# A state-space layer with a gated feed-forward, forward and backward, on one core: the next magnitudes loaded once the current ones are read, and the written order made anew

## The chip, the core and the metric

The kernel runs on one NeuronCore of a Trainium2 chip. TensorE (PE) multiplies matrices, with its weight loads (PEld) beside it; VectorE (DVE), ScalarE (ACT) and GpSimd (POOL) work on tiles of 128 partitions; SyncE (SP) issues DMAs, as ScalarE and GpSimd can too. Each engine runs its own list of instructions in order and waits on semaphores. PSUM holds what TensorE writes until another engine copies it out; such a copy is called an evacuation here. The metric is the device time of one execution in microseconds, the median of several.

## The reference

The forward pass is a layer norm, a state-space convolution of length 2048 per channel (512 channels, 128 states each) by FFT, a feed-forward layer of width 1792 that gates it, and a residual. The kernel returns the output and, from `jax.vjp`, eleven gradients for `grad_out`.

```python
def _A_ref(u, A_re, A_im, B_re, B_im, C_re, C_im, log_dt, Dskip):
    dt = jnp.exp(log_dt)[:, None]
    logdA = dt * (A_re + 1j * A_im)
    dB = dt * (B_re + 1j * B_im)
    P = jnp.exp(logdA[:, :, None] * l[None, None, :])
    K = jnp.einsum("dn,dnl,dn->dl", Cc, P, dB).real
    ...
    Yf = Uf * Kf[None, :, :, :]
    return y + u * Dskip[None, None, :]

def _B_ref(x, w1, w2):
    return jnp.einsum("bsf,fd->bsd", _silu(jnp.einsum("bsd,df->bsf", x, w1)), w2)

xn = _layernorm(x)
return x + _A_ref(xn, ...) * _silu(_B_ref(xn, B_w1, B_w2))
```

## The kernel before

Everything is written as generators ("streams"). Each `yield` ends a step. `PLAN` (L27 to L46) is seven strings of letters, one for each stage; `play` (L120) goes through a string and takes one step of the stream of that letter. So the strings are the program order of every engine and every DMA queue. `SLOTS` (L49) says which buffer of a pool each new tile takes, and `WAYS` (L65) says for each evacuation, stream by stream, whether ScalarE ("A", `nc.scalar.copy`, L116) or VectorE ("D", L117) makes it. The pool `pf` has three PSUM buffers, for the feed-forward, the turned tiles and the weight gradients, `pc` has two, for the convolution and the state-space part; a tile that takes a buffer waits until the tile before it there is evacuated.

The streams that matter here:

- Start. `gen_setup_loads` (1) loads the rows of x in five pieces, `gen_weight_loads` (0) W1 in three and W2 in two, `gen_param_loads` (p) loads the six parameter matrices by transposing DMAs. `gen_layer_norm` (6) makes xn on VectorE, `gen_rows_turned` (J) turns it on TensorE (L138), `gen_ffn_fwd` (F) multiplies by W1 (L763) and W2 (L780).
- Magnitudes. `gen_magnitudes` (7) computes |A| to 30 powers for every channel and stores it to DRAM as `Md`, eight pieces of 480 KB, one for each half (64 channels) of each of four blocks. Half number 2b+h is piece 2b+h.
- `gen_phases` (P) makes the phases of a half: two instructions on VectorE (L577, L580) and one on ScalarE (`sn`, L584).
- `gen_powers` (Q) is the function that is changed. For a half it loads the magnitudes into one part of `ds` (L597), multiplies phases by magnitudes in four multiplies (L611; two steps), which fill the table `E` (also in `ds`), the first powers in `Y` and a small `H`; it stores `E` to DRAM as `Ed` (L613), makes the other powers of `Y` in six multiplies and sums (L622, L624, L626), and stores `Y` as `Yd` (L628). `E`, `H` and the magnitudes have one buffer each; `Y` has two, one for each h.
- `gen_kernel_rows` (R) multiplies the table by C on VectorE (L646) and the powers by that on TensorE (L652), puts the rows of the convolution's kernel together in `KE` (L663, L667) and copies them to `Kb` in eight DMAs, one for each group of 16 channels (L683).
- `gen_conv_x` (X) and `gen_conv_fwd` (C) transform the input and the kernel (`dft_fwd`, L397: products L406, turns L420 to the tile `dB`, products L430 and L434) and multiply the spectra.
- Later stages: the backward convolution (D, B), the feed-forward gradients `gen_da` (A, L1168) and `gen_dx` (x, L1192), the state-space gradients (N, Y, V, T, S, Z), the weight gradients `gen_dw2` (w, L1231, with its turned tiles t) and `gen_dw1` (v, L1260, with the transposing loads of `dh_tok`, g, L1246), and the closing layer norm (i, k, m: loads L1280 and L1282, VectorE L1301 to L1323, ScalarE L1308). `gen_ssm_fold` (N) makes the tile `G21` of `pc` in two banks (L962) that ScalarE copies out (L965) before `gen_ssm_v` (V, L1020) can be read on. `gen_ssm_grads` (Z) stores its six results `gout` from GpSimd's queue (L1119).

Of the kernel before, what the change touches and what calls it, by code (L numbers as in the profile page):

```python
# [45 lines left out]
""".replace("\n", "").split("/")  # L46


SLOTS = dict(x.split("=") for x in """  # L49
fp.XT=01010101;pf.pf=012010210210120120102102012012012012012012012012012102102101210210210210210210202012012012012012102  # L50
102102102101202012102102102102102102120202102101210210210210210210212012012012012102102102102120120120102102120201201201
2020120210210201201201210;fp.hT=0101010101010101;dft.w8=21301203121030230123012320312301;pc.pc=0101011010101011010101010
101011010101010110101010101010101010101010101010101010101010101010101011010101010010101010101010101010101010101010101010
101010101010101010101010101010101010101010101010101101010101010101010101101010101010101011010111010101010101010010101010
10101010101010101;fp.ob=0101010;tbl.tv=01011101110101010101101010101110;tbl.ts=01010101010111010010101000100010;tbl.W=01
010110101110100101;dft.t4=010010101010;gate.g=30124567;gate.S=01;da.doT=01010101;da.dhT8=01201201;dftb.w8b=1010;da.dhT6=
10101010;go.go_s=01010101;go.go_r=010101;go.go_g=01010101;go.go_x=01201201;da.pd_s=101010101010;sb.YT=2012012012012012;s
b.Eb=01010101;sb.Gb=01010101;sb.Vb=0101010101010101;sb.Tp=0101010101010101;sb.Sa=1010;fw.h_in=01201201201201;fw.a_tok=10
101010101010;fw.o11=01201201201201;sb.g_acc=0101;fw.dh_tok=0120120;fw.o10=1010101;lw.pd_l=012301;lw.Gt=01230123;lw.m=010
101;lw.o1=12031203  # L60
""".replace("\n", "").split(";") if x)

WAYS = """J=DDADADAA;  # L65
F=ADAAAAAAADDAAADAAADAAAAAAAAAAADAAAAAAAAAAAAADDAAAAADAAADADDDAAADADDDAAAA;
X=AAAAAAAAAAAAAAAAAAAAAAAAAAAAAAAA;
U=AD;
R=AAAAAAAAAAADAADAAADAAADAAAAAAAAA;
C=ADDADAAAAAAAAAAAAAAADDAAAAAAAADDAAAAADAAAAADADAAADADDDADAAAAAAAA;  # L70
W=DDDDDDDDDDDDDD;
D=AAAADDAAAAAAAAADAAADAAAAAAAAAADAADAAAAAA;
d=DDADDAAD;
B=AAAAAAAAAAADAADAADAAAAAAAAAAAAAADAAADAAAAADAADAAAAAAADAA;
x=AADAADADDADA;
V=DAAADAAAAAAAAAAAADADAAADAAAAAAAAAAAAAAAAAAAAAAAAAAAAAAAAAAAAAAAA;
Y=DAAAAAAA;
w=DADADDAAAAAAAA;
v=AAADAADAAAADADAAAAAAAAAAAAAA"""


class Placed:
# [17 lines left out]
NX = len(X_EXP)  # L100
# [488 lines left out]
def gen_powers(k, b, h):  # L589

    nc, tbl = k.nc, k.tbl
    TT = nc.vector.tensor_tensor
    qe = lambda ap: ap.rearrange("p e c (q a) -> p e c q a", a=4)
    eq = lambda ap: ap.rearrange("p c q e a -> p e c q a")
    tab = k.ds[:].rearrange("p t d -> p (t d)")
    mag = tab[:, 5376:5376 + 64 * NX].rearrange("p (e d) -> p e d", d=64)
    nc.sync.dma_start(tab[:, 5376:5376 + 64 * NX], k.Md[2 * b + h])  # L597
    yield
    E = tab[:, 0:2688].rearrange("p (c q e a) -> p c q e a", c=2, q=16, a=4)
    Y = k.Y[h]  # L600
    H = tab[:, 7360:7744].rearrange("p (c q e a) -> p c q e a", c=2, q=16, a=4)
    k.E[b, h] = E
    for x0 in (0, 15):
        sn = k.sn.pop((b, h, x0))
        if x0 == 0:
            parts = ((E[:, :, :, 1:16, :], 0, 15),)
        else:
            parts = ((E[:, :, :, 16:NE, :], 0, 5), (Y[:, :, :, 1:8, :], 5, 12), (H, 12, 15))
        for o, i0, i1 in parts:
            m = mag[:, x0 + i0:x0 + i1, :].unsqueeze(2).to_broadcast([P, i1 - i0, 2, 64])  # L610
            TT(out=eq(o), in0=qe(sn[:, i0:i1]), in1=qe(m), op=ALU.mult)  # L611
        yield
    nc.sync.dma_start(k.Ed[b, h], tab[:, 0:2688])  # L613
    yield
    shp = [P, 16, 3, 8, 4]
    lo = lambda c: Y[:, c, :, 0:8, :].unsqueeze(2).to_broadcast(shp)
    hi = lambda c: H[:, c].unsqueeze(3).to_broadcast(shp)
    out = lambda c: Y[:, c, :, 8:32, :].rearrange("p q (k m) a -> p q k m a", m=8)
    for c, (x, y), op in ((0, ((0, 0), (1, 1)), ALU.subtract), (1, ((0, 1), (1, 0)), ALU.add)):
        m1 = tbl.tile(shp, BF16, name="m1", tag="tv", bufs=2)  # L620
        m2 = tbl.tile(shp, BF16, name="m2", tag="ts", bufs=2)
        TT(out=m1[:], in0=lo(x[0]), in1=hi(x[1]), op=ALU.mult)  # L622
        yield
        TT(out=m2[:], in0=lo(y[0]), in1=hi(y[1]), op=ALU.mult)  # L624
        yield
        TT(out=out(c), in0=m1[:], in1=m2[:], op=op)  # L626
        yield
    nc.sync.dma_start(k.Yd[b, h], Y[:].rearrange("p c q j a -> p (c q j a)"))  # L628
    yield
# [437 lines left out]
def gen_ssm_grads(k, b, sb):  # L1067
# [262 lines left out]
def kernel(ctx, tc, A_u, A_A_re, A_A_im, A_B_re, A_B_im, A_C_re, A_C_im, A_log_dt, A_Dskip, B_x, B_w1, B_w2, grad_out,  # L1330
# [53 lines left out]
    with ExitStack() as es_s:  # L1384
# [91 lines left out]
```

## Time and profile before

| | |
|---|---|
| three runs | 580.93, 579.06, 580.84 us; median 580.84 |
| the profiled execution | 584.31 us, of which 582.5 us are its span |
| granted TensorE clock, mean | 0.983 |
| DMA | 144.49 MB, mean 248 GB/s |
| magnitude load `ds<-Md` | eight of 480 KB on SyncE's queue, 6.2 us median from issue to landing |

The page of the profile lists, for the slowest core, the busy time of each engine, the span in 40 slices (a digit is the busy share in tenths), the chain that ended last, the costliest groups of instructions, and the DMA issues. A row of instructions reads: start, duration, engine, line, operation, out<-in, shapes, count, and in brackets the idle time of the engine just before it and what ended it. A row of waits reads: who waited, for whom, total, times, longest. "issue" there means that no releaser was found for the wait. SPq rows are DMA issues, with the time that SyncE's queue took to issue them.

### The profile page before, as it was taken

To read this page: it belongs to the slowest core of one execution; us is meant where nothing else is said; L and a number is where in the kernel's file an instruction comes from. 1 tells how busy PE (TensorE), PEld (TensorE's weight loads), DVE (VectorE), ACT (ScalarE), POOL (GpSimd) and SP (SyncE) were. 2 spreads that over 40 slices of the span, in tenths; PEclk is the share of its full clock that TensorE was granted. 3 is DMA by queue.
4 is the path that set the end of the run, shared out by engine and by line. 5 is a ranking of instruction groups with operands and counts; after the bars stand their busy time and mean duration, and the time that the engine had idled before them with its cause. 6 is when DMAs were issued, how large, how long until landed. Compare 5 with 4: busy or idle time off the path is not lost.

```text
span 582.5 us, 14494 instructions
## 1 busy us (share of the span) xinstructions
PE 528.8 (91%) x5983; PEld 395.7 (68%) x6008; DVE 521.9 (90%) x820; ACT 445.8 (77%) x542; POOL 77.6 (13%) x164
## 2 busy tenths in 40 slices
PE   0589998899999899999999999997899999999786
PEld 0355876586778675886587766765678797867564
DVE  7999998999999769999999999866999999991993
ACT  5989989899999669998888876752567686743563
POOL 4351101010101020000000000000000120333121
PEclk9989999999999999999999999999999999999798
DMA  8987897898977999779789999998899989999592
GB/s 245 283 317 194 260 245 252 266 291 220 356 218 253 322 283 365 230 254 289 243 258 289 262 297 282 222 182 220 227 230 220 211 240 251 198 227 235 119 270 97
DMA packets 156643, 144.49 MB, mean 248 GB/s; under 512 B 83488, under 2 KB 132896, under 8 KB 153504
## 3 DMA queue, kind: packets, MB, share of 16 engines
q1 hardware_dynamic: 146816, 120.74, 77.2%
q0 software_dynamic: 6640, 19.67, 10.0%
q10 hardware_dynamic: 3120, 3.15, 1.8%
q8 instruction: 47, 0.77, 0.5%
q14 instruction: 20, 0.16, 0.1%
HBM read 62.78 MB, written 59.25 MB: 209 GB/s over the span
## 4 chain that ended last, share of the span: by engine, by line
PE 45%; DMA 6%; DVE 4%; SPq 3%; issue 2%; ACT 1%; ACTq 0%; DVEq 0%
PE ps_w L1231 7%; PE ps_da L1168 7%; PE ps_w L1260 6%; PE ps_dx L1192 6%; DMA dh_tok<-DHd 4%; PE pt_t L138 3%; PE psS L1057 3%; PE ps_v L1020 3%; PE ps_i L451 2%; PE ps_i L464 2%; SPq L495 1%; PE ps_s L434 1%; PE ps_s L406 1%; DMA go_x<-in_A_u_dram 1%; PE pt_f L420 1%
## 5 line engine op out<-in xcount | busy, mean ns | idle before, releaser
L116 ACT CAST dA<-ps_s 128x1024 bf16<-128x1024 f32 x88 | 87.8, 1030 | 8.2 <-PE ps_s L434 3.8
L763 PE MATMUL ps_h<-XT,W 128*128 128x256 bf16 x448 | 59.6, 282 | 11.2 <-ACT hT L116 6.3
L116 ACT CAST Vb<-ps_v 128x672 bf16<-128x672 f32 x59 | 41.7, 728 | 24.2 <-PE ps_v L1020 15.7
L1260 PE MATMUL ps_w<-dh_tok,xn 128*128 128x256 bf16 x448 | 55.0, 280 | 5.6 <-ACT o L116 3.3
L763 PEld LDWEIGHTS <-W 128*128 128x128 bf16 x448 | 43.5, 101 | 19.6 <-issue 12.6
L1168 PE MATMUL ps_da<-doT,W 128*128 128x256 bf16 x448 | 56.1, 273 | 0.0
L1260 PEld LDWEIGHTS <-xn 128*128 128x128 bf16 x448 | 44.2, 100 | 12.6 <-issue 6.3
L1192 PE MATMUL ps_dx<-W,dhT 128*128 128x512 bf16 x224 | 51.2, 380 | 0.0
L780 PE MATMUL ps_o<-W,aT 128*128 128x512 bf16 x212 | 49.3, 379 | 1.6 <-ACT aT L771 0.6
L1231 PE MATMUL ps_w<-YD,a_tok 128*128 128x512 bf16 x211 | 49.1, 379 | 0.7
L116 ACT CAST dB<-ps_i 128x1024 bf16<-128x1024 f32 x39 | 39.0, 1021 | 11.2 <-PE ps_i L451 11.2
L1168 PEld LDWEIGHTS <-W 128*128 128x128 bf16 x448 | 41.4, 98 | 8.2 <-issue 2.1
L1171 DVE TENSOR_TENSOR dhT<-ps_da,dhT 128x512 bf16<-128x512 f32 x56 | 37.4, 682 | 5.1 <-PE ps_da L1168 5.0
L780 PEld LDWEIGHTS <-aT 128*128 128x128 bf16 x224 | 20.9, 98 | 26.0 <-ACT aT L771 2.6
L1192 PEld LDWEIGHTS <-dhT 128*128 128x128 bf16 x224 | 21.3, 98 | 24.2 <-issue 1.5
L1231 PEld LDWEIGHTS <-a_tok 128*128 128x128 bf16 x224 | 21.7, 98 | 23.5 <-ACT a_tok L1222 0.2
L477 DVE TENSOR_TENSOR cm<-sp_in,dA 128x2048 bf16<-128x2048 bf16 x24 | 29.3, 1220 | 3.9 <-ACT dA L116 2.8
L1020 PE MATMUL ps_v<-Gb,YT 128*128 128x168 bf16 x256 | 27.1, 238 | 5.6 <-ACT Vb L116 3.5
L584 ACT ACTIVATE sn<-V 128x1920 bf16<-128x1920 int16 x16 | 29.1, 1818 | 3.6 <-DVE ds L611 2.5
L116 ACT CAST o<-ps_w 128x256 bf16<-128x256 f32 (+1 forms) x34 | 14.7, 436 | 21.6 <-PE ps_w L1260 13.7
L1222 ACT ACTIVATE a_tok<-pt_t 128x1024 bf16<-128x1024 bf16 x28 | 29.0, 1039 | 2.7 <-PE pt_t L138 2.6
L1146 ACT ACTIVATE dhT<-dhT 128x2048 bf16<-128x2048 bf16 (+1 forms) x16 | 27.5, 1719 | 3.5 <-DMA dhT<-Hd 3.5
(242 smaller groups left out, 1238.9 us busy)
## 6 DMA issues: line engine op xcount, KB each, us to landing
Yd<-YD SPq DMA_DIRECT2D x8, 1024.0 KB, 5.5
sp_in<-Ud SPq DMA_DIRECT2D x8, 1024.0 KB, 7.7
h_in<-Hd SPq DMA_DIRECT2D x14, 512.0 KB, 5.2
Ed<-ds SPq DMA_DIRECT2D x8, 672.0 KB, 5.6
Eb<-Ed SPq DMA_DIRECT2D x8, 672.0 KB, 5.5
Hd<-hT POOLq DMA_DIRECT2D x8, 512.0 KB, 7.6
Ud<-dA SPq DMA_DIRECT2D x8, 512.0 KB, 9.7
KXd<-dA SPq DMA_DIRECT2D x4, 1024.0 KB, 4.1
```

Source lines behind the costliest of these rows:

```text
L116: return self.nc.scalar.copy(out=out, in_=in_)
L477: TT(out=t2[:], in0=b[:, :, gs], in1=a[:, 1:2, gs].to_broadcast([P, 2, n, P]), op=ALU.mult)
L584: nc.scalar.activation(out=sn[:, 0:n], in_=low, func=ACT.Sin, scale=-2 * PI_LO / 2.0 ** PB)
L763: nc.tensor.matmul(out=ps[:, j], lhsT=k.W1[:, dk, ft * P:ft * P + P], rhs=XTv[:, :, dk, :], start=(dk == 0), stop=(dk == DK - 1))
L780: nc.tensor.matmul(out=ps[:], lhsT=aT[:, ft, t * P:t * P + P], rhs=k.W2[:, ft, :], start=(ft == 0), stop=(ft == FT - 1))
L1020: nc.tensor.matmul(out=ps[:, u, 168 * c:168 * c + 168], lhsT=YT[:, c, q + u, :], rhs=Gb[:, q0 + q + u].rearrange("p w x -> p (w x)"), star ...
L1168: nc.tensor.matmul(out=ps[:, j], lhsT=k.W2[:, ft, dk * P:dk * P + P], rhs=dTv[:, :, dk, :], start=(dk == 0), stop=(dk == DK - 1))
L1171: nc.vector.tensor_tensor(out=dh[:, i0:i0 + 2, :], in0=ps[:], in1=dh[:, i0:i0 + 2, :], op=ALU.mult)
L1192: nc.tensor.matmul(out=ps[:], lhsT=dhs[ft // 8][:, ft % 8, t * P:t * P + P], rhs=k.W1[:, :, ft * P:ft * P + P], start=(ft == 0), stop=(ft ...
L1222: yield from turned(k, lambda t: h[:, t], k.T, a, lambda out, in_: k.nc.scalar.activation(out=out, in_=in_, func=ACT.Silu))
L1231: nc.tensor.matmul(out=ps[:], lhsT=at[:, t, :], rhs=k.do[:, t, :], start=(t == 0), stop=(t == k.T - 1))
L1260: nc.tensor.matmul(out=ps[:], lhsT=k.xn[:, t, dk * P:dk * P + P], rhs=dh[:, t].rearrange("p j n -> p (j n)"), start=(t == 0), stop=(t == k ...
```

## The change

In `gen_powers` the load of the magnitudes moves. Before, every half began with the load of its own. Now the first half alone does so, and every half but the last loads the next half's magnitudes as soon as its own multiplies (L611) are written, ahead of the store of the table `Ed`. The number of loads and their sizes are the same, and so is the number of steps.

```diff
-    nc.sync.dma_start(tab[:, 5376:5376 + 64 * NX], k.Md[2 * b + h])
-    yield
+    load = lambda i: nc.sync.dma_start(tab[:, 5376:5376 + 64 * NX], k.Md[i])
+    if (b, h) == (0, 0):
+        load(0)
+        yield
     E = tab[:, 0:2688].rearrange("p (c q e a) -> p c q e a", c=2, q=16, a=4)
...
             TT(out=eq(o), in0=qe(sn[:, i0:i1]), in1=qe(m), op=ALU.mult)
+        yield
+    if (b, h) != (3, 1):
+        load(2 * b + h + 1)
         yield
     nc.sync.dma_start(k.Ed[b, h], tab[:, 0:2688])
```

Beside it all seven strings of `PLAN` are new, and `SLOTS` and `WAYS` with them. The first lines of each:

```diff
 PLAN = """
-221325p5325515566767571677777766647701JJ70p7775076F6377766F76pF774770J786877J3F773177F06p6676643643F86853376F174F76FFFF6
...
+222315555166p567155737777617777p63677J710360734777p07J6760F3p67677J64FF7687J7F667F86676261F873776F03778FFFF47FF66667FF76
...
-WAYS = """J=DDADADAA;
...
+WAYS = """J=DDAADDAD;
```

Followed through the generators, letter by letter, the strings give every engine's list. Each list has the same steps as before (574 with work for TensorE, of which 477 stand in the same order; evacuations on VectorE 93 before, 94 now). The places of which the text below speaks, as the lists have them (half n is written Md*n*, Ed*n*, Yd*n*; da, dx, v, G are groups of L1168, L1192, L1020, L962):

| place | before | after |
|---|---|---|
| SyncE, start (x: pieces of the rows) | Ar, x0, x1, W1.0, x2, W1.1, Ai, W1.2, Br, Bi, W2.0, x3 | x0, Ar, x1, x2, Ai, W1.0, x3, W1.1, Br, Bi, W1.2, W2.0 |
| VectorE before the first xn | table steps (5), rows 0 and 1 of the statistics, L515, one table step | table steps (3), the two rows, table steps (3), L515 |
| SyncE, halves 1 to 3 | Ud0, Ed1, Yd1, load Md2, turn X1 (2), Kb0 (8), Ed2, Yd2, load Md3, Ud0 back, Ud1, Ed3, Yd3, load Md4 | Ud0, load Md2, Ed1, Yd1, turn X1 (2), Kb0 (8), load Md3, Ed2, Ud0 back, Ud1, Yd2, load Md4, Ed3 |
| SyncE, halves 6 and 7 | load Md6, KXd1, Ed6, turn X3 (2), Kb2 (8), Yd6, load Md7, Sd1, Ed7 | load Md6, ..., KXd1, load Md7, Ed6, turn X3 (2), Kb2 (8), Yd6, Sd1, Ed7 |
| TensorE, second fold | dx6.0, ..., G1.0, da7.5, dx6.1, v2.0, da7.6, G1.1, v2.1 | dx6.0, G1.0, da7.4, G1.1, da7.5, dx6.1, v2.0, v2.1 |
| evacuations of v2.0, v2.1 | ScalarE, both | VectorE, both |
| TensorE, closing (dW1 groups w1, dW2 groups w2, turned tiles T) | w1_3.2, w1_3.3, T11, T11, w1_4.0, w1_4.1, w2_10, T12, w1_4.2 | T11, w1_3.2, w1_3.3, w2_10, T11, w1_4.0, w1_4.1, T12, w1_4.2 |
| ScalarE, closing | ..., o10 of w1_4.0, T11, first L1308, o10 of w1_4.1, o11 of w2_10 | ..., o10 of w1_3.3, first L1308, o11 of w2_10, T11, o10 of w1_4.0 |
| SyncE, closing (pairs of `dh_tok` f.0, f.1) | ..., 5.0, h13, L1280 and L1282 for rows 3 and 4, 5.1, row 5, 6.0, 6.1 | 5.0, rows 0 to 2, 5.1, rows 3 and 4, 6.0, row 5, 6.1 |

More of the change, by code (lines that the diff above doesn't have):

```diff
@@ new lines @@
+347674678F73F586F47688758/XXJPFJFFFXXXFXFXPXFQPFPFXFFPFFPFFFFPPFFFFF9FQJUUXFQQXJPXXQRQQXQQQFRFQPRRFRXFXFRXXPRFFPRRFFFPQF
+UQRXXFFQFXFQFQPQQFUQFQFQRFFXFQXPXFPFXQRPXFRXRPRRRRRXPQRPFFFRPFRRRRRXFRFRXCQXXXQFXQQXQRQFQQRFQXXFRRUXFPRRQCRPFCPPFCFCCFCC
+PCFQFJFQCQCCFQQFCQPFQCRRCCQQRCCFPXCXFQPCPJFXRFCFXRCFCPFCXFXFFFRCFRFQFRCFRFFRXFCXPCRRQQXFXRFCQCFRQFQQQRCRCRRQCQRCRRRCFQPC
+XCXRRFCRRJPPXPXXRQJFXRPXQCQFQXFXFXQPQCRRQFQPQCPCRXFCCRFFQFCCCFCPCCFFRFFUFFCQCFFFCRCRCFCQRCFCCCRJCCRCQCXPXFXPCQCXRPCRCQXC
+FXFCRQQPCRQPJCFRQCRCRFXCQPQCCXFFRFRXRQRXRFFXQCXRCPFFCRRFCFCRRCRFFFXXCQQCFCCFQFQQXFRXRRFRCCQCFUFXCQCQRCCQCRRRCRJCCRQRRCRJ
@@ new lines @@
+CRCCCRUCFCRCCRCRRFCRRFCC/CFCFCGGCGFGCCCGFFFCCFGCCCGGCGFCCFFCFGFCCCCGCFGGFWCCGFGCCCGHFCFCGHFCCFCGGFHCFCCGGCFCGCGCGCCCFCWG
+CHWHWHWHCWCCCWWCDDGWCHCLCWMCWWWWDDWWDWDDWDWWWWLMWCDWDDWDLGDMDLMLWWM/DDEDDDDaaasdooEdWDdoDdDABAADooAABADsBDADAAaDAABAlABB
+BBDDAABABAsDDAAaoBAABBBADODABBABOEBBABABDBBoDDBxsBDBBxBoBxBAAdBBBOoBAsAlDBOABxBdOEDBDoOlBxBaDxOoOBxOxODDBBDxxDBlABBsxBoB
+ABBxoBAADBOAAOaBaoDBBBBBoDDBaAABBDAoDAdDBBAADBAdBABBAEAABABsBBAAODOABoOABBDBABEADODoDOxoDBAlDsOBoADDOAxAdBDDBOAoAdBADABB
+BoxBAoOADsDxBABOOBBADBDOlaBoAAxOBDBDooxBBxBBaBAOxDxBABDoBDOsODBDADxBEBOBAAOdBOBoBABxxOAoAaBdABAoBBExBOAsBBBDDOBAaOBAxBAB
@@ L53 @@
[L53 to L57, printed above, removed]
+fp.XT=01010101;pf.pf=012020120120120120102102102102102102102101201201201201210210201201201020120120121210210210210210120
@@ L58 @@
+010110101101011010;dft.t4=010010101010;gate.g=30127456;gate.S=01;da.dhT8=01201201;da.dhT6=01010101;da.doT=10101010;dftb.
+w8b=1010;go.go_s=01010101;go.go_r=010101;go.go_g=01010101;go.go_x=01201201;da.pd_s=101010101010;sb.YT=0120120120120120;s
 b.Eb=01010101;sb.Gb=01010101;sb.Vb=0101010101010101;sb.Tp=0101010101010101;sb.Sa=1010;fw.h_in=01201201201201;fw.a_tok=10
-101010101010;fw.o11=01201201201201;sb.g_acc=0101;fw.dh_tok=0120120;fw.o10=1010101;lw.pd_l=012301;lw.Gt=01230123;lw.m=010
+101010101010;fw.o11=01201201201201;fw.dh_tok=0120120;sb.g_acc=0101;fw.o10=0101010;lw.pd_l=012301;lw.Gt=01230123;lw.m=010
@@ L71 @@
 W=DDDDDDDDDDDDDD;
[L72 to L79, printed above, removed]
+D=AAAADDAAAAAAAAADAAAAAAAAAAAAAAAAAADAAAAA;
+d=DDDAADAA;
+B=AAAAAAAAAAADAADAAAAAAAAADADAAAAAAAAAAAAADAAADAAAAAAADAAA;
+x=AADDDAADAAAA;
+V=ADDDAAADDDAAAAAADDAAAAADDAAAAAAAAAAAAAAAAAAAAAAAAAAAAAAAAAAAAAAA;
+Y=AAAAADAA;
@@ L82 @@
+w=AAAAAAAADDAAAA;
+v=DDDAAADDAAAAADDAAAAAAAAAAAAA"""
 class Placed:
```

39 lines of the change are left out of this document (16 added, 23 removed).

## The prediction

> **What bounds the kernel now.** I read the page first: the busy line, then TensorE's 40 slices.
>
> ```profile
> span 582.5 us, 14494 instructions
> PE 528.8 (91%) x5983; PEld 395.7 (68%) x6008; DVE 521.9 (90%) x820; ACT 445.8 (77%) x542; POOL 77.6 (13%) x164
> PE   0589998899999899999999999997899999999786
> ```
>
> TensorE idles 53.7 us (582.5 - 528.8), and by its slices at four places: the start, a shallow dip at slices 7 and 8, one at slice 28, and the end. No engine bounds it all. Windows cut at these places, busy microseconds in the order PE, PEld, DVE, ACT, POOL, then granted clock, DMA share and GB/s:
>
> ```profile
> 7.08:43.41 36.33, 20.85 (x138) 14.00 (x140) 35.23 (x87) 32.12 (x50) 15.38 (x19) 0.91 0.99 306
> 43.41:106.00 62.59, 56.27 (x616) 41.28 (x619) 58.84 (x77) 58.31 (x63) 7.44 (x9) 1.00 0.88 247
> 106.00:194.30 88.30, 84.71 (x1126) 64.86 (x1133) 87.14 (x110) 83.40 (x93) 8.68 (x11) 1.00 0.87 265
> 250.00:375.00 125.00, 124.51 (x1541) 91.03 (x1539) 121.06 (x160) 101.96 (x102) 6.48 (x12) 1.00 0.87 264
> 425.00:538.70 113.70, 113.12 (x1189) 88.56 (x1198) 99.33 (x176) 73.49 (x115) 23.31 (x42) 1.00 1.01 225
> 538.70:553.40 14.70, 11.35 (x67) 7.47 (x67) 14.39 (x40) 7.72 (x12) 1.61 (x3) 0.77 0.59 122
> ```
>
> VectorE bounds the start (35.23 of 36.33). Between 43 and 194 us VectorE and TensorE are both nearly full. From 250 to 375 and from 425 to 538 us TensorE is the bound, so what is won before 250 is kept there. The magnitudes are read on VectorE at L611, inside the co-bound stretch.
>
> **The edit itself.** VectorE's waits at L611, its instructions around the longest, and the SyncE queue before it, start and duration first:
>
> ```profile
> DVE ds L611 <- issue: 2.8, 1, 2.8
> DVE ds L611 <- DMA ds<-Md: 1.0, 2, 0.6
> 98.94 0.68 DVE L580 TENSOR_SCALAR V<-V 128x960 int32<-128x960 int32 x1
> 102.39 1.56 DVE L611 TENSOR_TENSOR ds<-sn,ds 128x1920 bf16<-128x1920 bf16 x2 [2.77 <-issue]
> 73.95 0.34 SPq L628 DMA_DIRECT2D Yd<-YD  x1
> 74.39 0.81 SPq L597 DMA_DIRECT2D ds<-Md  x1
> 86.14 5.84 SPq L683 DMA_DIRECT2D Kb<-KE  x8
> 92.09 0.54 SPq L613 DMA_DIRECT2D Ed<-ds  x1
> 93.15 0.89 SPq L597 DMA_DIRECT2D ds<-Md  x1
> DMA to landing us min/median/max: 9.2/9.2/9.2
> DMA to landing us min/median/max: 3.1/6.2/9.2
> ```
>
> The profile puts two waits down to the magnitude load and calls the third "issue". The last two rows are the landing times of the load at 93.15 alone and of all eight loads. 93.15 + 9.2 = 102.35, and VectorE starts at 102.39: the third wait is the load's too. So the load costs VectorE 2.77 + 1.0 = 3.8 us. Its place in the queue shows why: it stands behind the store of the powers (74.39 comes right behind 73.95, a store that waits for the last sum at L626), though the old magnitudes were read long before.
>
> After the change the load stands ahead of the table's store (L613) and of the powers' store. For half 3 that is right behind the eight Kb copies, at 86.14 + 5.84 = 92.0 in place of 93.15. This is only 1.2 us sooner; the larger part is what it is no longer queued behind. Landing after 3.1 to 6.2 us it is there at 95.1 to 98.2, ahead of the 99.62 (98.94 + 0.68) at which VectorE comes free; after another 9.2 it is there at 101.2 and 1.6 us of wait stay. The bytes in flight decide:
>
> ```profile
> 88.00:92.00 4.00, 2.47 (x23) 1.49 (x22) 4.00 (x6) 3.80 (x5) 1.12 (x1) 1.00 0.36 83
> 92.00:95.00 3.00, 2.61 (x47) 2.17 (x43) 2.97 (x4) 2.68 (x3) 0.91 (x1) 1.00 0.90 311
> Ed<-ds SPq DMA_DIRECT2D x8, 672.0 KB, 5.6
> 105.94 0.62 PE L434 MATMUL ps_s<-dB,F 128*64 128x512 bf16 x4 [2.06 <-DVE dB L117]
> ```
>
> At 92.0 the engines have been at 0.36, and the 311 GB/s behind it come from the stores that will now follow; I take the early landing. Late next is the table's store: the next L611 writes the table that L613 reads. Moved from 92.09 to about 92.5, it lands 5.6 later, at 98.1: 1.5 us of cover. The wait moves nobody else on SyncE: load and store are released by the same group of multiplies.
>
> What TensorE gets of it: its 2.06 us at 105.94 wait for a copy (dB) that stands behind the late multiplies on VectorE. I count that, and the 0.6 of the earlier wait (the larger of the two named ones), which lies ahead of it in the same window: **-2.7 us**. The last wait, 1.0 - 0.6 = 0.4, falls in the window in which TensorE has 84.71 of 88.30; there I count nothing. Bounds: 0 (all wait comes back) and -3.8 (all of VectorE's).
>
> By the Trainium skill (DMA: Bandwidth & Descriptors, Anatomy of one DMA) a DMA takes about 2.0 us plus its bytes over 436 GB/s, a fit for the GpSimd path; 480 KB would make 3.1 us, an estimate, the load of 93.15 would have been there at 96.3, and this term would be zero. The trace shows 3.1 as the shortest of the eight and 9.2 for this one, so I go by the trace.
>
> **The new order: start.** 477 of TensorE's 574 steps keep their order, and 93 evacuations on VectorE become 94, so the work of each engine is the same to within a microsecond or two.
>
> ```profile
> 0.75 1.27 SPq L370 DMA_TRANSPOSE Ar<-in_A_A_re_dram  x1
> 2.08 1.03 SPq L350 DMA_DIRECT2D x_sb<-in_A_u_dram  x2
> 7.08 0.69 DVE L382 BATCH_NORM_STATS2 st<-x_sb 128x6 f32<-128x512 bf16 x1 [0.43 <-DMA x_sb<-in_A_u_dram]
> 11.02 1.03 PE L138 MATMUL pt_t<-ident,xn 128*128 128x128 bf16 x8 [11.02 <-DVE xn L390]
> ```
>
> The first rows of x now go ahead of Ar: 2.08 - 0.75 = 1.3 us sooner, and statistics start at 5.8 in place of 7.08. Before the first xn VectorE still has the same small table steps, of which some now follow the statistics; I take 0.8 of the 1.3: **-0.8 us** (bounds 0 and -1.3). The first third of W1 moves behind more of x and behind Ai; if it is late for the first product, that eats this term, hence the bound 0.
>
> **The new order: first products (slice 28).**
>
> ```profile
> 401.51 0.38 PE L962 MATMUL G<-GE,FO 128*128 128x32 bf16 x8
> 401.97 1.86 ACT L965 CAST Gf<-G 128x2048 bf16<-128x2048 f32 x1 [9.41 <-PE G L962]
> 404.51 0.45 PE L1020 MATMUL ps_v<-Gb,YT 128*128 128x168 bf16 x4 [2.62 <-ACT Vb L116]
> ```
>
> The second bank of the fold (401.51) is made two da groups, a dx group and a v group behind the first, and the tile of both holds one of the two buffers of pc all that time. ScalarE waits 9.41 us for it, and the evacuation of v that TensorE needs stands behind it on ScalarE. In the new order the second bank comes one da group behind the first and ahead of the dx group, and the next two evacuations of v go to VectorE. The wait of 2.62 loses its cause: **-2.6 us**. The upper bound is 0: the next load of YT is late instead, since the queue ahead of it on SyncE is the same and v comes to it that much sooner. The lower bound is -2.6 too, as no other wait stands there with this cause.
>
> **The new order: closing part.**
>
> ```profile
> 537.75 0.69 DVE L1301 SCALAR_TENSOR_TENSOR pd_l<-pd_l,ds 128x512 bf16<-128x512 bf16 x1 [10.01 <-DMA dh_tok<-DHd]
> 540.76 1.52 ACT L1308 ACTIVATE pd_l<-pd_l,m,rstd 128x512 bf16<-128x512 bf16 x2 [5.79 <-DVE m L1304]
> 542.59 3.57 PE L1260 MATMUL ps_w<-dh_tok,xn 128*128 128x256 bf16 x16 [3.30 <-ACT o L116]
> 566.18 1.91 PE L1260 MATMUL ps_w<-dh_tok,xn 128*128 128x256 bf16 x16 [2.27 <-DMA dh_tok<-DHd]
> 573.05 0.69 DVE L1323 TENSOR_TENSOR o<-o,ds 128x1024 bf16<-128x1024 bf16 x1 [0.54 <-ACT ds L1308]
> 577.26 0.37 ACT L116 CAST o<-ps_w 128x256 bf16<-128x256 f32 x1 [1.38 <-PE ps_w L1260]
> L1260 PE MATMUL ps_w<-dh_tok,xn 128*128 128x256 bf16 x448 | 55.0, 280 | 5.6 <-ACT o L116 3.3
> DMA to landing us min/median/max: 4.8/6.6/11.9
> ```
>
> The row at 573.05 ends VectorE's closing chain, which runs with one hole from 537.75 to 573.74 (36.0 us); that at 577.26 is the last evacuation; the last row is the landing of the transposed loads of dh_tok. The profile names such a load as what ended the 10.01 us ahead of the chain; the chain's buffers, though, lie where gout lay, so I take the stores of gout to be in it too. In the new order the second half of the sixth pair of dh_tok loads and the first of the seventh stand ahead of loads that are blocked by the chain, so the wait of 2.27 should go. Against it: ScalarE now reaches the first L1308 with three tiles queued behind it (dW2's eleventh block, a turned block, a dW1 block), all three buffers of pf; before, a dW1 block and a turned one were ahead of it. TensorE stops sooner by a dW1 block (16 matmuls, 55.0 / 28 = 1.96 us) and a turned one (8 matmuls of half the width, a quarter: 0.5), and goes on 0.2 later, as the evacuation it waits for is twice as wide: 3.30 + 2.7 = 6.0. Sum -2.27 + 2.7 = **+0.4 us**; bounds +2.7 (the late load stays late) and -5.6 (chain so early that neither wait is left).
>
> The clock behind that stop is left out of the term: 0.77 of full speed over 14.7 us, 0.23 x 14.7 = 3.4 us, is paid now as well. By the Trainium skill (TensorE: Matmul & The Clock Gate, The HAM clock gate) an idle window of about 3.4 us halves the clock; the trace agrees after 3.30 us, and a stop of 6.0 would add at most one more such window, 1.7 us by that estimate.
>
> **New waits.** I cannot see those that the new order makes. The longest wait of the co-bound stretch that no part above touches is this, and I add one of its size, **+1.1 us** (bounds 0 and +4, some four of them, as 97 of 574 steps moved):
>
> ```profile
> PE ps_k L652 <- ACT dB L116: 1.1, 1, 1.1
> ```
>
> Sum: -2.7 - 0.8 - 2.6 + 0.4 + 1.1 = -4.6 us. The profiled execution took 584.31, so 579.7 there; the three runs shown have a median of 580.84, 3.5 less, so 576.2.
>
> **Rivals.** One: the waits only change their names. The table's store has 1.5 us of cover and the next YT load none; if both land late, the terms -2.7 and -2.6 go, and -0.8 + 0.4 + 1.1 = +0.7 stays: 581.5. For it speaks the landing of 9.2 us in a full queue; against it that nothing of size stands ahead of the moved load. Two: the closing chain also starts earlier against TensorE, and its term is midway between +0.4 and -5.6, -2.6; the sum is -7.6: 573.2. For it: two dh_tok loads leave the stretch in which the gout stores are under way; against it: that those stores are what the chain waits for is inferred. Three, slower: the stores land later, as the same loads now go just ahead of them. The closing chain of 36.0 us starts only then. It has at most 577.63 - 573.74 = 3.9 us to spare, and the other terms sum to -5.0, so a slip of L costs L - 3.9 - 5.0: it decides from 8.9 us, which lies between the median and the longest landing of one such load (6.6 and 11.9), and at 11.9 gives +3.0: 583.8. Against it: the loads are moved earlier, not later.
>
> **Chances.** Forecast 0.46, rival one 0.22, two 0.20, three 0.12. A measurement here tells about 0.3% (1.7 us) from no change: faster is below 579.1, slower above 582.6. Forecast (574 to 579.5 by itself) and rival two are faster but for 0.03; rival one is the same in 0.19, slower in 0.03; three is slower: 0.63, 0.22, 0.15. The range leaves out most of three and the best of two, where all gains reach their bounds: 571.5 to 582.5.
>
> **What would show it.** Right: L611 no longer waits for any load, its landing is under 7 us at half 3, TensorE's wait at the first L434 of that block is gone; TensorE's first turn near 10.2; no wait over 1 us at L1020 where the second bank of the fold is made; a stop of about 6 us at L1260 behind the first L1308 and none for dh_tok later. Wrong: L611 still waiting for a load or for the table's store, the closing chain (first L1301) starting later than 538, or new waits of TensorE of over 1 us between 106 and 375.

## The result and the profile after

| | before | changed |
|---|---|---|
| median of 12 runs each | 580.42 us (578.18 to 584.75) | 575.03 us (570.23 to 576.90) |
| the profiled execution | 584.31 us | 576.90 us |
| its span, mean granted TensorE clock | 582.5 us, 0.983 | 575.1 us, 0.981 |

The ratio of the times is 0.9896, with a 95% interval of 0.9868 to 0.9924: faster by 5.4 us. The forecast was 576.2, in a range of 571.5 to 582.5. The two profiled executions are 7.4 us apart, more than the medians, because that of before is 3.9 us over its median and that of after 1.9. Ratios here and below leave out the few executions that took over 1.5% longer than their kernel's fastest (one of e10 took 693.41 us, at a granted clock of 0.755). From the page of the changed kernel:

```profile
span 575.1 us, 14488 instructions
PE 528.4 (92%) x5982; PEld 396.0 (69%) x6008; DVE 523.5 (91%) x821; ACT 442.6 (77%) x541; POOL 79.0 (14%) x164
PE   0788998999999999999999999999999999899895
```

TensorE's busy time is what it was (528.8), so between these two profiles the gain is idle time: the dips at slices 8 and 28 are gone, while slice 7 keeps its 8. Busy time also holds what a lower granted clock costs; the third number from the end of a row of windows is that clock, and it matters at the fold below. Since both kernels give TensorE nearly the same busy time, I cut each trace where TensorE had done 40, 110, 200, 360, 385 and 460 us of it. A row shows the bounds, the length and TensorE's busy time; length minus busy is its idle time in that stretch. Before:

```profile
0.00:64.00 64.00, 40.00 (x306) 27.11 (x309) 59.66 (x135) 55.41 (x72) 21.12 (x71) 0.95 0.88 262
64.00:140.10 76.10, 70.03 (x882) 52.35 (x886) 72.28 (x91) 71.09 (x82) 7.44 (x9) 1.00 0.90 256
140.10:235.50 95.40, 89.92 (x1201) 67.92 (x1204) 85.52 (x104) 83.17 (x94) 11.26 (x16) 1.00 0.89 294
235.50:396.90 161.40, 160.01 (x1965) 119.89 (x1963) 149.91 (x203) 127.18 (x129) 6.48 (x12) 1.00 0.88 251
396.90:427.10 30.20, 25.01 (x229) 17.42 (x229) 23.39 (x34) 14.77 (x20) 0.00 (x0) 0.94 0.94 241
502.50:577.20 74.70, 68.86 (x579) 51.59 (x581) 57.21 (x140) 38.68 (x64) 18.56 (x33) 0.95 0.90 209
```

Changed:

```profile
0.00:62.10 62.10, 40.05 (x297) 26.56 (x300) 59.03 (x134) 54.39 (x72) 21.57 (x71) 0.95 0.88 268
62.10:135.80 73.70, 69.95 (x884) 53.77 (x887) 71.10 (x90) 70.73 (x81) 7.18 (x9) 0.98 0.85 253
135.80:230.90 95.10, 89.96 (x1170) 67.48 (x1174) 85.89 (x103) 80.52 (x92) 12.44 (x16) 1.00 0.92 298
230.90:393.10 162.20, 160.00 (x1988) 119.87 (x1985) 149.59 (x201) 130.69 (x135) 6.48 (x12) 1.00 0.86 254
393.10:419.40 26.30, 25.05 (x247) 17.57 (x246) 25.46 (x37) 13.85 (x19) 0.00 (x0) 1.00 1.04 266
494.80:568.80 74.00, 68.37 (x581) 51.03 (x585) 58.21 (x140) 36.18 (x62) 18.49 (x33) 0.95 0.79 206
```

Idle time goes from 24.0 to 22.1 at the start, from 6.1 to 3.8 in the stretch of the long magnitude wait, from 5.5 to 5.1 and from 1.4 to 2.2 in the next two, from 5.2 to 1.3 at the fold, and from 5.8 to 5.6 at the end. The stretch left out (385 to 460 us of work) has 0.4 in both.

The magnitudes in the changed kernel (the line numbers behind the load are two to five higher than before). SyncE's queue, the landing time of the load at 90.59 and then of all eight, VectorE at the first multiply of half 3, and TensorE:

```profile
84.35 6.14 SPq L688 DMA_DIRECT2D Kb<-KE  x8
90.59 0.54 SPq L597 DMA_DIRECT2D ds<-Md  x1
```
```profile
DMA to landing us min/median/max: 5.4/5.4/5.4
DMA to landing us min/median/max: 3.5/4.7/8.1
```
```profile
98.52 1.55 DVE L613 TENSOR_TENSOR ds<-sn,ds 128x1920 bf16<-128x1920 bf16 x2
```
```profile
92.51 0.61 PE L406 MATMUL ps_s<-Kb,TF 128*128 128x128 bf16 x8 [2.35 <-DMA Kb<-KE]
103.90 0.62 PE L434 MATMUL ps_s<-dB,F 128*64 128x512 bf16 x4
502.63 0.51 PE L1117 MATMUL pt_g<-ident,gout 128*128 128x128 bf16 x6 [1.71 <-DVE gout L1111]
534.48 3.57 PE L1265 MATMUL ps_w<-dh_tok,xn 128*128 128x256 bf16 x16 [3.24 <-ACT o L116]
```

The load goes out right behind the copies of the kernel rows, lands in 5.4 us, and the multiply has no bracket: nothing was waited for. TensorE's wait of 2.06 at L434 is gone, but it waits 2.35 us at 92.51 for those copies, and VectorE, which had waited 2.77 for the load, now waits 2.04 at 95.65 for the product behind them. At the end there is a new wait of 1.71, the stop behind the closing chain is as long as before (3.30), and the later one of 2.27 for `dh_tok` is gone.

### The profile page after: what moved, and what is told of

The parts are those of the page before. It is cut to its first block, busy times and chain, and to the rows that moved or that the text cites. A ratio compares the mean times of both kernels' runs of the same rounds, so it can differ in the third digit from the quotient of the medians.

```text
span 575.1 us, 14488 instructions
## 1 busy us (share of the span) xinstructions
PE 528.4 (92%) x5982; PEld 396.0 (69%) x6008; DVE 523.5 (91%) x821; ACT 442.6 (77%) x541; POOL 79.0 (14%) x164
## 4 chain that ended last, share of the span: by engine, by line
PE 57%; DVE 15%; ACT 7%; issue 7%; DMA 7%; SPq 4%; POOL 2%; ACTq 0%; DVEq 0%; POOLq 0%
PE ps_da L1173 8%; PE ps_dx L1197 7%; PE ps_w L1236 7%; PE ps_w L1265 6%; PE ps_o L785 3%; PE ps_h L768 3%; PE ps_i L451 3%; PE pt_t L138 3%; PE ps_s L406 3%; DMA sp_in<-Ud 3%; PE ps_i L464 3%; PE ps_v L1025 2%; PE psS L1062 2%; PE ps_k L657 2%; PE ps_s L434 2%
## 5 line engine op out<-in xcount | busy, mean ns | idle before, releaser
L116 ACT CAST dA<-ps_s 128x1024 bf16<-128x1024 f32 x90 | 89.1, 1029 | 9.6 <-PE ps_s L434 4.1
L785 PE MATMUL ps_o<-W,aT 128*128 128x512 bf16 x212 | 50.8, 387 | 1.7 <-issue 0.5
L116 ACT CAST Vb<-ps_v 128x672 bf16<-128x672 f32 x54 | 38.5, 732 | 17.6 <-PE ps_v L1025 13.7
L116 ACT CAST dB<-ps_i 128x1024 bf16<-128x1024 f32 x41 | 40.7, 1027 | 9.1 <-PE ps_i L451 9.1
L1236 PEld LDWEIGHTS <-a_tok 128*128 128x128 bf16 x224 | 21.6, 98 | 23.2
L406 PEld LDWEIGHTS <-TF 128*128 128x128 bf16 x384 | 24.9, 100 | 12.1 <-ACT TF L288 4.4
L479 DVE TENSOR_TENSOR sp_in<-sp_in,dA 128x2048 bf16<-128x2048 bf16 x24 | 29.3, 1223 | 0.6
```

The source lines that it names most:

```text
L116: return self.nc.scalar.copy(out=out, in_=in_)
L406: nc.tensor.matmul(out=ps[:, j], lhsT=k.TF[:, 8 * h + j, c, :], rhs=U(8 * h + j), start=True, stop=True)
L479: TT(out=b[:, :, gs], in0=b[:, :, gs], in1=a[:, 0:1, gs].to_broadcast([P, 2, n, P]), op=ALU.mult)
L785: nc.tensor.matmul(out=ps[:], lhsT=aT[:, ft, t * P:t * P + P], rhs=k.W2[:, ft, :], start=(ft == 0), stop=(ft == FT - 1))
L1236: nc.tensor.matmul(out=ps[:], lhsT=at[:, t, :], rhs=k.do[:, t, :], start=(t == 0), stop=(t == k.T - 1))
```

## The experiments

All ratios are to the kernel before, run beside each (there its medians are 581.2 to 582.0); an interval is 95%. "Idle" is TensorE's idle time in microseconds in the five stretches from 0 to 40, 110, 200, 360 and 385 us of its work, worked out as above from each kernel's own trace.

| kernel | us | ratio (interval) | 0-40 | 40-110 | 110-200 | 200-360 | 360-385 |
|---|---|---|---|---|---|---|---|
| before | 580.42 | 1 | 24.0 | 6.1 | 5.5 | 1.4 | 5.2 |
| changed | 575.03 | 0.9896 (0.9868-0.9924) | 22.1 | 3.8 | 5.1 | 2.2 | 1.3 |
| e12, changed again | 574.40 | 0.9900 (0.9868-0.9932) | 22.1 | 3.5 | 4.9 | 2.0 | 1.2 |
| e1, new order, late load | 594.68 | 1.0227 (1.0190-1.0264) | 22.1 | 15.3 | 12.4 | 2.2 | 1.3 |
| e2, old order, load earliest | 588.39 | 1.0137 (1.0095-1.0179) | 23.4 | 8.9 | 7.8 | 1.6 | 4.2 |
| e7, old order, load at the store | 584.90 | 1.0050 (1.0017-1.0084) | 23.2 | 4.6 | 8.0 | 1.7 | 5.5 |
| e10, as e7, two loads late | 580.03 | 0.9982 (0.9950-1.0013) | 23.6 | 4.0 | 5.6 | 1.1 | 4.2 |
| e5, the fold alone | 576.82 | 0.9911 (0.9876-0.9947) | | | | | 1.6 |
| e8, e7 and the fold | 581.45 | 1.0001 (0.9969-1.0033) | 23.8 | 4.2 | 8.4 | 1.3 | 3.3 |
| e9, the start alone | 582.31 | 1.0010 (0.9981-1.0040) | 22.8 | 5.4 | 5.4 | 1.4 | 4.9 |
| e3, changed, Ar first | 574.46 | 0.9875 (0.9832-0.9919) | 22.3 | 4.0 | 5.8 | 1.8 | 1.2 |
| e6, changed, sum early | 573.84 | 0.9879 (0.9820-0.9937) | 22.5 | 3.4 | 4.9 | 1.8 | 1.2 |
| e11, as e6, products later | 575.56 | 0.9896 (0.9851-0.9941) | 22.1 | 3.9 | 4.6 | 2.2 | 1.2 |
| e13, three parts, old order | 573.72 | 0.9877 (0.9834-0.9920) | 21.8 | 2.9 | 6.2 | 1.1 | 1.9 |

Of e5 the fold alone is read, since its profiled execution took 583.59 us, 6.8 over its median. How much is scatter shows where kernels run the same order: changed and e12 differ by 0.3 at most in these stretches, but by 1.7 in the last one (5.6 and 3.9); the five kernels with the old start and the old stretch behind it (before, e2, e7, e8, e10) lie between 23.2 and 24.0 in the first, and those with the old fold (before, e2, e7, e9, e10) between 4.2 and 5.5.

**Is it the load or the order? (e1, e2)** e1 is the changed kernel with the load behind the store of the powers, e2 the kernel before with the load behind the multiplies. In the kernels that move the load in the old order (e2, e7, e8, e10, e13) the first half alone begins with its own load, as in the changed kernel; that part of the diffs is left out.

```diff
 e1
-    if (b, h) != (3, 1):
-        load(2 * b + h + 1)
-        yield
+    if (b, h) != (3, 1):
+        yield
     nc.sync.dma_start(k.Ed[b, h], tab[:, 0:2688])
...
     nc.sync.dma_start(k.Yd[b, h], Y[:].rearrange("p c q j a -> p (c q j a)"))
+    if (b, h) != (3, 1):
+        load(2 * b + h + 1)
     yield
 e2
             TT(out=eq(o), in0=qe(sn[:, i0:i1]), in1=qe(m), op=ALU.mult)
+        if x0 == 15 and (b, h) != (3, 1):
+            load(2 * b + h + 1)
         yield
```

> The new order with the load of the magnitudes put back behind the store of the powers; each engine's order is otherwise that of the changed kernel. Theory (the place of the load is what counts): VectorE waits at the first multiply of some halves again, 3 to 4 us in all as before (2.77 + 1.0), and 2.7 us of it come back at the end: 577.7 us, midway between 575.0 (changed) and 580.4 (before). Rival (the new order gives the load enough time by itself): no wait of VectorE at that line, 575.0 us within 0.9.

> The old order with nothing changed but the load, which is issued right behind the multiplies that read the magnitudes of before. Theory: the waits of VectorE at the first multiply (2.77 + 1.0) and TensorE's 2.06 for the copy behind it go: 580.4 - 2.7 = 577.7 us. Rival (the waits only change their names, on the kernel rows or the store of the table): 580.4 us within 0.9, with a new wait of 1 to 3 us between 85 and 110 us. The changed kernel shows such a one: 2.35 us for the kernel rows at 92.51.

e1 is 19.7 us over the changed kernel (594.68 - 575.03), not 2.7. In the new order the store of the powers stands further back in SyncE's queue, behind the load and stores of the spectra, and a load behind it is very late. VectorE in e1, and the landing times of its eight loads:

```profile
111.03 1.16 DVE L613 TENSOR_TENSOR ds<-sn,ds 128x1920 bf16<-128x1920 bf16 x1 [11.21 <-DMA ds<-Md]
```
```profile
DMA to landing us min/median/max: 3.3/5.8/13.4
```

So the new order needs the early load. The converse is the surprise: e2, with the early load in the old order, is 6.4 us slower than before. VectorE has no wait for magnitudes there, but TensorE has three of 2.7 to 3.4 us for the transposed tile dB. SyncE's queue around the first, and the group of the three waits:

```profile
77.02 3.63 SPq L415 DMA_TRANSPOSE dB<-dA  x1
83.38 0.33 SPq L597 DMA_DIRECT2D ds<-Md  x1
83.77 3.36 SPq L415 DMA_TRANSPOSE dB<-dA  x1
```
```profile
PE ps_s L430 <- DMA dB<-dA: 8.8, 3, 3.4
```

The queue issues in order, and the load is not free to go until the multiplies of half 2 end at 83.36. From 80.65 (77.02 + 3.63) SyncE stands at it, and the second transpose of the pair stands behind it.

**The place that the prediction meant (e7).** The load one step later, directly ahead of the store of the table.

```diff
+    if (b, h) != (3, 1):
+        load(2 * b + h + 1)
     nc.sync.dma_start(k.Ed[b, h], tab[:, 0:2688])
     yield
```

> The old order with the load one step later than in e2_load_alone: right ahead of the store of the table, behind the transposes of the spectra and the copies of the kernel rows, as the prediction placed it. Theory (e2_load_alone was slow because the load, waiting for its multiplies, held up the transposes behind it): the three waits of 2.7 to 3.4 us at L430 are gone, VectorE no longer waits for the magnitudes, and the time is 2.7 us under the kernel before (ratio 0.995). Rival (the early load itself slows the transfers around it): waits at L430 or for the kernel rows of 2 us or more stay, ratio 1.000 to 1.014.

Half 3 does what was forecast: idle time from 40 to 110 us of work falls from 6.1 to 4.6. But the kernel is slower, 1.005, and the stretch behind it shows why: 8.0 in place of 5.5. SyncE's queue at half 6, TensorE behind it, and the landing times of the two transposes, in e7:

```profile
163.63 0.32 SPq L597 DMA_DIRECT2D ds<-Md  x1
164.00 1.24 SPq L617 DMA_DIRECT2D Ed<-ds  x1
165.41 9.32 SPq L415 DMA_TRANSPOSE dB<-dA  x2
```
```profile
175.47 0.60 PE L430 MATMUL ps_s<-dB,F 128*128 128x512 bf16 x2 [3.52 <-DMA dB<-dA]
```
```profile
DMA to landing us min/median/max: 6.2/8.1/10.0
```

The same place in the kernel before:

```profile
164.46 0.32 SPq L613 DMA_DIRECT2D Ed<-ds  x1
166.44 6.18 SPq L415 DMA_TRANSPOSE dB<-dA  x2
```
```profile
DMA to landing us min/median/max: 5.0/5.8/6.5
```

With a load of 480 KB put just ahead of them the two transposes take 9.32 us to issue, not 6.18, and the later one lands after 10.0 us, not 6.5. Over the 4 us behind TensorE's wait of 3.52 the granted clock is 0.65, which idle time does not count. The rival's ratio holds (1.000 to 1.014), but of the three waits of e2 only this one is left over 1 us. The Trainium skill (DMA: Bandwidth & Descriptors, Queues, rings and completion order) says that each DMA engine takes the descriptors of one ring in order; these rows agree with it.

**The two loads in question (e10).** Only the loads of halves 5 and 7 go back behind the store of the powers.

```diff
+    late = (b, h) in ((2, 0), (3, 0))
+    if (b, h) != (3, 1) and not late:
+        load(2 * b + h + 1)
     nc.sync.dma_start(k.Ed[b, h], tab[:, 0:2688])
...
+    if late:
+        load(2 * b + h + 1)
```

> The kernel of e7_load_at_store, but the two loads that would go just ahead of transposes (those of halves 5 and 7, issued 2.8 and 1.8 us ahead of them) stay behind the store of the powers, as before the change. Theory (the transposes of dB behind a load and a store land late, 9.5 and 10.0 us for the second of a pair in place of 7.5 and 6.5, and TensorE waits for them at L430): no wait of over 1 us at L430, TensorE's idle time in its work from 110 to 200 us falls from 8.0 to about 5.5, the gain of 1.5 to 2.7 us at half 3 stays, ratio 0.995 to 0.998. Rival (early loads cost as much elsewhere in that stretch): ratio 1.002 or more, idle time there over 7.

In e10, the second and third stretch:

```profile
63.60:137.50 73.90, 69.95 (x883) 52.09 (x882) 71.71 (x90) 70.13 (x81) 7.24 (x9) 1.00 0.93 264
137.50:233.10 95.60, 90.02 (x1195) 67.50 (x1193) 85.17 (x104) 82.92 (x94) 11.31 (x16) 1.00 0.89 289
```

Idle time 4.0 and 5.6: the gain of half 3 stays (2.1 against before) and the loss is gone. The ratio, 0.9982, is just over the theory's range, and its interval takes in 0.995 as well as no change; but it lies apart from that of e7 (0.9950 to 1.0013, 1.0017 to 1.0084). So the two loads ahead of the transposes are what made e7 slow. The landing times say so too: without the load the later transpose at half 6 lands after 6.5 us again, and at half 4 after 6.7 in place of 9.5. In the changed kernel the load of half 5 stands behind the transposes (issued at 128.82, they at 121.32) and that of half 7 goes out 4.2 us ahead of them (162.04 and 166.28), which leaves a wait of 0.86.

**The start (e3, e9).** e3 is the changed kernel with Ar ahead of the first rows of x; e9 is the kernel before with the first string of the new `PLAN` (the fifth J step and the nineteenth F step open the second string; two buffers of `pf` change places).

```diff
 e3
-222315555166p567155737777617777p63677J36
+222315555p166567155737777617777p63677J36
 e9
-221325p5325515566767571677777766647701JJ
+222315555166p567155737777617777p63677J36
```

> The changed kernel with one step moved back: the transposed load of the first parameter (Ar, 1.24 us of the queue) again ahead of the first rows of x. Theory: the statistics start 1.2 to 1.3 us later, VectorE bounds the start, and all of it stays: 576.3 us, with TensorE's first turn at 10.2 in place of 8.95. Rival (the other steps of the new start give the gain): 575.0 us within 0.6, TensorE's first turn under 9.5.

> The kernel before with the new order of the first part alone (up to the first powers), and the load of the magnitudes where it was. Theory: TensorE is 1.9 us ahead at 62 us, as in the changed kernel, and 0.8 to 1.9 us of it are left at the end: ratio 0.997 to 0.9985. Rival (the lead is lost again at the wait for the magnitudes of half 3, which does not move with it): no lead after 110 us, ratio 1.000.

VectorE's first statistics and TensorE's first turn in the changed kernel:

```profile
4.28 0.69 DVE L382 BATCH_NORM_STATS2 st<-x_sb 128x6 f32<-128x512 bf16 x1
8.95 0.61 PE L138 MATMUL pt_t<-ident,xn 128*128 128x128 bf16 x4 [8.95 <-DVE xn L390]
```

and in e3:

```profile
6.37 0.69 DVE L382 BATCH_NORM_STATS2 st<-x_sb 128x6 f32<-128x512 bf16 x1 [2.10 <-DMA x_sb<-in_A_u_dram]
10.36 1.03 PE L138 MATMUL pt_t<-ident,xn 128*128 128x128 bf16 x8 [10.36 <-DVE xn L390]
```

Ar first makes the statistics 2.1 us later and the first turn 1.4, and costs nothing by 40 us of TensorE's work: 22.3 against 22.1. The reason is in the waits: in the changed kernel the early first turn is followed by a second wait of 1.37 for xn, and both together (10.3) are as long as e3's one (10.4). So neither early event is the gain. The new start has a mean idle time of 22.2 (eight rows of the table, 21.8 to 22.8) and the old one of 23.6 (five, 23.2 to 24.0): the new order of the start is worth 1.4 us there, and which of its steps gives it stays open. Alone (e9) it is not told from no change (0.9981 to 1.0040). Its trace doesn't show the loss that the rival named: e9 is 1.2 us ahead of the kernel before at 40 us of work and still 1.9 at 110 (138.2 against 140.1). So whether the lead reaches the end is not shown.

**The fold (e5, e8).** In the kernel before three N steps move: the second bank one da group behind the first, and its copies with it.

```diff
-NAxTTAxVANNAVTTN
+NANNxNTTAxVAAVTT
```

> The kernel before with three steps moved: the second bank of the second fold stands one da group behind the first, ahead of the dx group, and its two copies follow. Theory: ScalarE's wait of 9.41 falls under 7, TensorE's wait of 2.62 for the evacuation of v goes: 580.4 - 2.6 = 577.8 us. Second reading (the wait of 0.99 ahead of it goes as well): 580.4 - 3.6 = 576.8 us. Rival (the next load of YT is late in its place): 580.4 us within 0.9, with a wait of 2 us or more for YT or its evacuation between 400 and 415 us.

> The load of e7_load_at_store and the fold of e5_fold_alone together in the old order. Theory (the two gains add, since TensorE has no slack between them): 2.7 + 3.6 = 6.3 us under the kernel before, ratio 0.989, which is what the whole change brought. Rival (what the load wins in front is lost ahead of the fold): the fold's gain alone, ratio 0.991 to 0.994.

e5 at the fold, TensorE's waits there in e8, and the same in the kernel before:

```profile
398.20:424.80 26.60, 25.02 (x245) 17.34 (x244) 25.47 (x36) 14.93 (x20) 0.00 (x0) 1.00 1.05 263
```
```profile
PE ps_v L1024 <- DMA YT<-Yd: 1.7, 1, 1.7
```
```profile
PE ps_v L1020 <- ACT Vb L116: 3.4, 3, 2.6
PE ps_v L1020 <- DMA YT<-Yd: 1.0, 1, 1.0
```

Three moved steps bring 0.9% (0.9911, some 5.2 us), more than the first theory's 2.6; the 3.6 of the second reading lies in the interval (3.1 to 7.2). So does what the whole change brings: on the time the fold alone is not told from it. Idle time at the fold is 1.6 (26.60 - 25.02), not 5.2. The 2.6 is gone in both. These 3.6 us are not all that the wait cost: in the kernel before the granted clock of this stretch is 0.94, in e5 1.00, and 0.06 of 30.2 us is 1.8 us, an estimate. The two together would be 5.4. In e8 YT came late, 1.7 us: the fear of the first rival is real, but the changed kernel and e13 are at 1.3 and 1.9 in all. Since e8 carries the loss of e7 too, it ends where it began, outside both ranges. Against e7, run beside it, the fold brings 3.4 us (584.90 - 581.45).

**A wait taken away (e6, e11).** In the changed kernel the copy of a sum (S) moves ahead of the copy of YT (Y); e11 also moves the first product of the kernel rows (C) two blocks of h back.

```diff
 e6, e11
-vTVtZZYYhvvTS
+vTVtSZZYYhvvT
 e11
-CRPFCPPFCFCCFCC
+RPFPPFFFCCCCCCC
```

> The changed kernel with one step moved forward: the copy of a sum (L1065) that VectorE waits for 2.23 us at 498.40 stands ahead of the copy of a turned block of YT on ScalarE, right behind its matmuls. Theory: TensorE's wait of 1.71 at 502.63 goes, and the stores of gout land as much sooner, so the closing chain moves with it: 1.7 us under the changed kernel (ratio to the kernel before 0.987). Rival (TensorE only comes sooner to the stop behind the first L1313): the stop grows from 3.24 to 4.9 and nothing is won, ratio 0.990.

> The kernel of e6_sum_early with the first product of the kernel rows two blocks of h later on TensorE (2 x 0.9 us of work that does not wait for the copies). Theory: TensorE's wait of 2.35 us for the copies at 92.51 falls to about 0.6 and 1.2 to 1.7 us stay to the end, ratio to the kernel before 0.985. Rival (VectorE, which waits 2.04 us for the same product, is no sooner): no gain on the changed kernel run beside it.

> The changed kernel as it is, beside the other two on the same chip: ratio 0.990 within its interval of before. If it comes out over 0.992 or under 0.987, the small differences of the other runs are not told apart either.

TensorE and VectorE in e6, then TensorE in e11:

```profile
500.12 0.51 PE L1117 MATMUL pt_g<-ident,gout 128*128 128x128 bf16 x6 [1.21 <-DVE gout L1111]
```
```profile
495.89 0.69 DVE L1102 TENSOR_TENSOR gout<-g_t,dt 128x512 bf16<-128x512 f32 x1 [1.74 <-ACT YT L116]
```
```profile
95.73 1.86 PE L406 MATMUL ps_s<-Kb,TF 128*128 128x128 bf16 x16 [2.13 <-ACT dA L116]
```

Both theories fell. With the sum's copy ahead, VectorE still waits 1.74, and now the profile names the copy of YT; TensorE's 1.21 is no less than the 1.28 that e12 has without the step moved. The wait for the kernel rows became one for ScalarE's evacuation of the products before it. None of e6, e11, e12 is told from the changed kernel: their intervals all hold 0.990. No version was found that beats it.

**The parts together (e13).** The start of e9, the loads of e10 and the fold of e5 in the otherwise old order; the diffs are those above.

> The old order with three parts of the change: the new start of e9_start_alone, the early loads of e10_two_late and the fold of e5_fold_alone; the other steps, the closing part among them, stand where they stood before. Theory (these three are the change): TensorE's idle time falls by 1.1 + 2.1 + 3.5 = 6.7 us against the profile of before, ratio 0.988 to 0.990, as the changed kernel. Rival (the load of YT is late again, as in e8_load_and_fold, and the rest of the new order matters): the fold gives 1.7 in place of 3.5, ratio 0.992 to 0.995.

The ratio is 0.9877 (0.9834 to 0.9920), and the interval takes in the theory's 0.988 to 0.990. The second, third and fifth stretch in e13:

```profile
61.80:134.70 72.90, 69.98 (x882) 52.39 (x886) 71.65 (x91) 70.83 (x82) 7.35 (x9) 1.00 0.93 267
134.70:230.90 96.20, 89.99 (x1197) 67.77 (x1199) 85.42 (x104) 83.07 (x93) 11.20 (x16) 1.00 0.88 290
392.00:418.90 26.90, 25.05 (x249) 17.29 (x249) 25.06 (x36) 15.95 (x21) 0.00 (x0) 1.00 1.04 263
```

Three local parts bring the whole gain. The other new places, the closing part among them, are not needed for it; whether the start and the load are, beside the fold, was not tried: by themselves e9 and e10 are not told from no change, and e5 is not told from the whole.

## Why the prediction was right, point by point

| term | predicted | the two profiles | alone or in parts |
|---|---|---|---|
| the edit | -2.7 (0 to -3.8) | -2.32 (40-110) | -2.1 (e10); not told from 0 on the time |
| start | -0.8 (0 to -1.3) | -1.95 (0-40) | -1.4 (means); not told from 0 on the time (e9) |
| fold | -2.6 (0 to -2.6) | -3.94 (360-385) | -3.6 (e5); -5.2 on the time |
| closing part | +0.4 (+2.7 to -5.6) | -0.21 (460 to the end) | not tried |
| new waits | +1.1 (0 to +4) | +0.47 (110-360) | |
| sum | -4.6 | -7.95 | -5.4 in the median |

TensorE's last matmul ends 8.4 us sooner (577.2 and 568.8): 8.0 of idle time and 0.4 of busy time. What lies behind it grows from 5.3 to 6.3 us (span minus the last bound), so the span is 7.4 us shorter.

- **The sum.** That -4.6 came near is in part luck. The term of the fold was too small, by 1.0 us of idle time and 2.6 on the time (e5); the stop at the end was forecast to grow and did not; and the gains of the edit and of the start, which the traces show, are not told from nothing on the time of a kernel with one of them alone (e10, e9).
- **The edit.** Right in mechanism: no wait at the multiplies, a landing of 5.4 us at half 3, L434 without its wait. The issue at 90.59 is near the 92.0 of the working. What came late next was not the table's store but the copies of the kernel rows (2.35), which the reckoning of cover had not looked at. That new wait is a little longer than the 2.06 that went. So the size agrees in the changed kernel by luck: TensorE's other waits between 40 and 110 us of work, each under 0.7, fall from 3.6 to 1.2 in sum, and the prediction counted on 0.6 of that. In e10 no wait for the copies came and the other waits sum to 3.6 as before; what went there is the wait at L434, 2.1 us. One sentence failed: "The wait moves nobody else on SyncE". It looked at half 3 alone. At half 6 the transposes are behind, and in the old order they cost what half 3 wins (e7). The forecast held because the new order sets them apart, which the prediction had not asked for.
- **The start.** The reason fell: the first rows ahead of Ar are not what helps (e3). The first turn at 8.95 was even sooner than the 10.2 given. What the traces show instead is another set of waits behind the first turn: before, 2.82, 1.35 and 6.25 us (the last for `hT`), in the changed kernel 2.93, 2.02 and 4.08 (the last for the table `TF`).
- **The fold.** The mechanism is shown by moving it alone. The bound of -2.6 was too tight: it left out the 1.0 us for YT ahead of the same work, which comes and goes (1.0 before, 1.3 in e7 and none in e10 with the same steps there, 1.7 in e8, none in the changed kernel), and the clock behind the stop.
- **The closing part.** The stop did not grow to 6.0; it is 3.24. The prediction let TensorE come 2.7 us sooner to it; the new wait of 1.71 ahead of it took most of that, so what should have been paid at the stop was paid at L1117. The 2.27 for `dh_tok` went, but it is a poor term: of the kernels with the old closing part e2, e7, e8, e9, e10 and e13 show no wait of over 0.9 us in its place. The chain did start sooner than 538, and the stores of gout are what it waits for, as was inferred:

```profile
529.42 0.69 DVE L1306 SCALAR_TENSOR_TENSOR pd_l<-pd_l,ds 128x512 bf16<-128x512 bf16 x1 [4.52 <-DMA out_dram<-gout]
```

- **New waits.** Between 110 and 360 us of work idle time grows by 0.47, and no new wait of over 1 us stands there. The two new waits that are longer, 2.35 and 1.71, came elsewhere and count in other rows.
- **The rivals.** One (waits only change names) did not come true as a whole, though both of its halves exist: in e8 for YT, in the changed kernel for the kernel rows. Three did not come: the chain starts 8.3 us sooner (529.42 against 537.75). Two's time (573.2) is nearly as near to 575.03 as the forecast's (576.2 is 1.2 off, 573.2 1.8), but for another reason: the fold, not the chain.

## What to carry to other kernels

A DMA that is moved forward in an in-order queue has two prices, and both are at every place where it is issued, not at the longest wait alone: how long the queue stands at it until its own release, and how much later the transfers behind it land. An edit and an order that was made with it are one thing: here the new order with the late load (e1) and the old order with every load early (e2, e7) were slower than the kernel before. Three steps moved at one place, found as a long wait of an evacuating engine behind a two-bank tile, were worth nearly as much as the whole change. What a long wait costs is not its length alone: the work behind it can run at a lower clock.

## What the runs showed of the hardware

- The landing time of one and the same load of 480 KB runs from 3.1 us to 13.4 (e1). The latter was issued at 97.62, right behind a load of 1024 KB, two stores of 512 KB and one of 1024 KB.
- A pair of transposing DMAs behind a load of 480 KB and a store of 672 KB took 9.32 us to issue, 6.18 behind the store alone.
- Two executions of the same kernel differ by 1.7 us of TensorE's idle time in the closing stretch alone (5.6 in the changed kernel, 3.9 in e12). A term of that size can't be read from one profile.
- Behind a stop of TensorE the granted clock can fall, and the length of the stop doesn't decide it. Over the 4 us behind the wait of 2.62 at the fold it was 0.58 in the kernel before, 0.50 in e7 and e9, 0.65 in e2, and 1.00 in e10. It was 0.57 behind the 2.35 in the changed kernel, 0.50 behind the stops of 3.30 and 3.24 near the end of the kernel before and of the changed one, and 1.00 behind 2.92 in e10 and 3.42 in e2. The prediction's sentence on an idle window of about 3.4 us is too simple for this. At 0.58, 4 us of work lose 0.42 x 4 = 1.7 us, an estimate.
